# HGRN2 scan and gated MoE on one core: score matmuls cut to 64 by 64 tiles for all pairs, first pair as one MoE unit, one more pair turned by DMA, and a new order of steps

## The chip, the cores and the metric

The kernel runs on one core of one Trainium2 chip. The metric is the device time of one execution in microseconds (us), as the median of three runs. A profile of one execution gives the trace that is read here; its span runs from the program's first to its last instruction.

The engines are named as in the profile: PE is TensorE's matmuls, PEld its weight loads, DVE is VectorE, ACT is ScalarE, POOL is GpSimd and SP is SyncE, whose queue (SPq) issues nearly all transfers.

## The reference

Four batches, eight heads, 768 tokens, head width 48. A gated recurrence gives x, and a two-layer MoE-like block with h * cos(h) follows:

```python
def _attn_ref(q, k, v, f_logit):
    f = 1.0 / (1.0 + np.exp(-f_logit))
    state = np.zeros((B, H, D, D))
    for t in range(S):
        state = f[:, :, t, :, None] * state + einsum('bhd,bhe->bhde', k[:, :, t], v[:, :, t])
        y[:, :, t] = einsum('bhd,bhde->bhe', q[:, :, t], state)

def _moe_ref(x, w_in, w_out):      # x: 3072 x 384, w_in: 384 x 2048, w_out: 2048 x 384
    h = x @ w_in
    g = h * np.cos(h)
    return g @ w_out
```

Inputs and output are 32-bit floats.

## The kernel before

**Tiling.** The recurrence is done in chunks. 256 tokens of one batch are a *pair* (two chunks of 128 tokens): 12 pairs, three for each batch, n = 0 to 11. A token pair (even, odd) shares a partition, so that a chunk has 64 partitions. The MoE block works on *units* m of 256 tokens; `UNITS = [128, 128] + [256] * 11` lets pair 0 be units 0 and 1, so that pair n is unit n + 1 from n = 1 on.

**Steps.** `describe` makes a graph of named steps, each with a function that emits its instructions. For a pair n:

- `f`, `k`, `q`, `v` load the inputs on SP (halves `.0` and `.1`, four heads each, for pairs 0 and 1; f0.0 goes on ACT's queue).
- `ex`, `ln`, `fx`, `fy` (ACT), `ad` (POOL) make the log decays; `cum` (PE, L374 and L380) sums them along the tokens; `eb` and `ei` (ACT, L391 and L395) are the exponentials of the sums.
- `qa` (L341), `ka` (L351), `qm`, `km` (L404) scale q and k into the tile `qk`: on DVE or POOL for pairs 0 and 1, on POOL for the others. `vb` and `vt` (L197) cast and place v.
- `tq`, `tk` turn q and k for one half u of the heads. For pairs outside `TURN_QK = range(5, 12)` they are four PE transposes each (L435), and `qkt` (DVE or ACT) copies the result out of PSUM. For pairs in `TURN_QK` there is one step `tq{n}.{u}` on SP, a DMA transpose from `qk` to `qkt` (L424), and no copy.
- `sc` (PE, L456) are the scores; `am` (DVE, L461) masks them; `ps` (PE, L479) are the products k times v of the state, on 64 by 64 tiles; `st` and `sz` (DVE, L497 and L503) carry and decay the state.
- `y` and `yi` (PE, L531) give the pair's x, transposed; `xe` (ACT or DVE, L197) copies it out.

For a unit m: `h{m}.{j}{s}` (PE, L579) is a slice of the first product, six matmuls with 256 columns, or twelve with 128 columns for a unit of 128 tokens; `co` (ACT, L584) is the cosine and `g` (DVE, L561) the gate; `o{r}.{s}` (PE, L595) is a quarter of the second product for 128 tokens, four matmuls of 384 columns; `ot` copies it out and `out` stores it. The last store is split in two halves, `.0` and `.1`.

The weights come in four quarters each: `w0.i` (w_in) and `w1.i` (w_out) are loads of 768 KB on SP into a slot of the `g` pool, and `wc0.i`, `wc1.i` cast them on POOL or ACT.

`zf0` to `zf53` (PE, L264) are matmuls on zeros that fill TensorE's time at the start; their result is not used.

**Order.** Nothing is scheduled at run time. The string `ORDER` lists all steps with an engine letter (T PE, S ACT, V DVE, G POOL, Y SP) and the slots that their results take, e.g. `tk4.0:T` or `tq5.1:Y2`. `emit` goes through it and issues each step on its engine, so that every engine runs its own steps in that order, and waits by semaphores for what a step reads and for the last reader of the slot it writes. PSUM has four tiles of two banks, numbered 0 to 7 as slots; a step for scores or for h takes a whole tile. SBUF pools have the slot counts in `SLOTS` (three for `qk`, five for `qkt` and `g`). SP's queue is in order too: a load that waits for its slot holds all behind it.

**Scores before.** The step `sc` takes each of eight blocks (two head pairs a, two chunks g, two heads r). For a turned pair the 128 key tokens are cut in two: 16 matmuls with 64 stationary columns. For the others one matmul has all 128 stationary columns: 8 matmuls.

Of the kernel before, what the change touches and what calls it, by code (L numbers as in the profile page):

```python
# [41 lines left out]
zf18:T3 cum1.1:T3 zf19:T4 zf20:T4 zf21:T4 tq0.1:T0 cum1.0:T1 qm0.0:G zsz.2:G eb1.0:S1 vt0.3:S2
k1.0:Y ei1.0:S0 ex3:S zf22:T4 zf23:T4 zf24:T4 zf25:T4 zf26:T4 ps0.1:T4,5 ps0.0:T tk0.1:T v1:Y1 f2:Y0
qkt0.1:V0 eb1.1:S ln3:S0 ei1.1:S ka1.0:G q1.0:Y0 tq0.0:T ka1.1:G km1.1:G0 zvt.1:G vt0.0:S ad3:G1
vt0.1:G q1.1:Y vb1:S1 qkt0.0:V1 vt0.2:G zsz.1:G ex2:S w0.1:Y0 w0.0:Y1 k3:Y0 q3:Y1 w0.3:Y2 ln2:S1
vt1.2:S1 fy3:S zf27:T6 zf28:T6 zf29:T6 zf30:T6 zf31:T6 zf32:T6 sc0.0:T0 sz0.01:V2 sz0.00:V w0.2:Y3
ad2:G0 vt1.0:G km1.0:V vt1.3:G wc0.1:G am0.0:V0 zf33:T6 zf34:T6 yi0:T4 sc0.1:T2 am0.1:V1 st0.11:V
sz0.11:V3 wc0.0:G k2:Y1 zf35:T6 zf36:T6 zf37:T6 zf38:T6 ps1.1:T6,7 tk1.0:T0 ps1.0:T zf39:T1 zf40:T1
zf41:T1 cum3:T1 fy2:S ei3:S0 fx3:S ka3:G eb3:S2 vt1.1:S fx2:S km3.0:G1 qa3:G qm3.0:G km3.1:G qm3.1:G
w1.0:Y0 qa1.0:V st0.10:V qa1.1:V qm1.0:V wc0.2:G ka2:G q2:Y2 tk1.1:T2 zf42:T3 zf43:T3 y0:T3 tq1.0:T  # L50
xe0.1:S0 sz0.10:V st1.00:V st1.01:V qm1.1:V v2:Y1 zf44:T5 zf45:T5 zf46:T5 zf47:T5 zf48:T5 tq1.1:T
cum2:T1 sz1.00:V1 qkt1.0:V0 eb2:S0 xe0.0:S ei2:S1 qkt1.1:V1 km2.0:G0 km2.1:G zf49:T5 sc1.0:T4
sz1.01:V zf50:T0 zf51:T0 sc1.1:T2 h0.01:T0 st1.11:V sz1.11:V2 am1.1:V0 wc1.0:G qa2:G zf52:T6 zf53:T6
h0.00:T co0.0:S0 qm2.1:G am1.0:V1 h1.01:T2 h1.00:T co1.0:S1 y1:T6,4 yi1:T g0.0:V1 xe1.1:V1 st1.10:V
qm2.0:G vb2:G1 sz1.10:V g1.0:V4 w1.2:Y3 xe1.0:S tk3.0:T5 h2.01:T0 tq3.0:T w1.3:Y0 qkt3.0:V0 v3:Y0
f4:Y0 h2.10:T6 h2.00:T sc3.0:T4 tq3.1:T2 tk3.1:T h2.11:T wc1.2:G wc1.3:G vt2.1:G1 wc0.3:S vb3:G0
co2.0:S1 am3.0:V0 g2.0:V2 h2.20:T4 h2.21:T h0.11:T0 co2.1:S0 qkt3.1:S1 co2.2:S1 sc3.1:T2 w1.1:Y3
g2.1:V am3.1:V1 g2.2:V h0.10:T h1.11:T6 h1.10:T h2.30:T2 tk2.1:T4 tk2.0:T5 co0.1:S0 co1.1:S2 g0.1:V
g1.1:V h2.31:T o2.0:T0 co2.3:S0 tq2.1:T vt3.2:G2 vt3.1:G tq2.0:T o0.0:T1 o3.0:T6 o1.0:T7 qkt2.0:S2
vt2.0:S g2.3:V qkt2.1:V3 sc2.0:T2 ex4:S o3.2:T o0.2:T am2.0:V2 ln4:S1 ps2.0:T4 sc2.1:T2 vt2.3:G  # L60
ps2.1:T am2.1:V3 st2.01:V st2.00:V sz2.01:V1 sz2.00:V wc1.1:S f5:Y2 ex5:S ln5:S0 o1.2:T o2.3:T
o3.3:T o0.3:T o2.2:T q4:Y2 ps3.0:T4,5 ps3.1:T zsz.0:G vt2.2:G ad4:G0 yi2:T2,3 y2:T vt3.3:G sz3.01:V0
sz3.00:V o1.3:T cum4:T4 v4:Y0 vt3.0:G ad5:G0 fy4:S eb4:S0 st3.11:V fx4:S k4:Y1 fy5:S qa4:G qm4.0:G1
fx5:S ei4:S1 o0.1:T o2.1:T o3.1:T xe2.0:V1 st3.10:V sz3.10:V1 qm4.1:G sz3.11:V xe2.1:V ot2:V0
h3.00:T2 o1.1:T cum5:T0 ei5:S0 eb5:S2 k5:Y0 h3.01:T ot0:V1 vb4:G0 ka4:G y3:T4,5 yi3:T q5:Y1 h3.10:T0
h3.11:T co3.0:S0 xe3.0:V0 xe3.1:V ot1:V2 ot3:V3 co3.1:S2 g3.0:V4 h3.21:T4 h3.20:T co3.2:S1 h4.21:T6
h4.20:T g3.1:V ka5:G km4.0:G co4.2:S0 km4.1:G vt4.1:G2 qa5:G h4.11:T2 h4.10:T g3.2:V co4.1:S2
h4.31:T0 k6:Y2 qm5.1:G0 h4.30:T vt4.0:G vt4.2:G km5.1:G f6:Y1 v5:Y0 v6:Y1 f7:Y0 tq4.0:T4 tq4.1:T5
out3:Y tk4.0:T tk4.1:T co4.3:S1 g4.2:V2 h3.31:T6 h3.30:T qkt4.1:S0 qkt4.0:V1 g4.1:V o5.1:T4 co3.3:S0
o5.2:T o5.0:T o4.1:T5 g4.3:V g3.3:V ps4.1:T0,1 ps4.0:T st4.01:V st4.00:V sc4.1:T2 sc4.0:T6 am4.1:V0  # L70
am4.0:V1 sz4.00:V0 sz4.01:V qm5.0:G vt4.3:G st4.10:V tq5.1:Y2 sz4.10:V2 o5.3:T o4.2:T km5.0:G o4.0:T
o4.3:T ex6:S ln6:S0 vb6:G0 ad6:G0 ex7:S cum6:T2 y4:T3,6 tq5.0:Y3 yi4:T ot5:S3 st4.11:V sz4.11:V
vb5:G1 fx6:S ln7:S1 ei6:S0 eb6:S1 xe4.1:S1 o6.2:T4 out5:Y ad7:G0 ka6:G km6.0:G1 km6.1:G vt5.0:G2
vt5.1:G ps5.0:T2 ps5.1:T xe4.0:S st5.01:V sc5.0:T6 am5.0:V0 out0:Y k7:Y0 q6:Y1 q7:Y2 fy6:S fx7:S
f9:Y2 sc5.1:T0 cum7:T3 o6.3:T o6.1:T vt5.3:G h4.01:T6 h4.00:T st5.00:V am5.1:V1 sz5.01:V0 vt6.3:G1
qa6:G eb7:S0 ot4:S1 ka7:G ei7:S1 ps6.1:T3,5 ps6.0:T sz6.01:V1 sz5.00:V sz6.00:V v7:Y0 co4.0:S0
qm6.0:G h5.00:T0 h5.01:T co5.0:S1 vt5.2:S g4.0:V st6.11:V fy7:S h5.31:T2 h5.30:T o6.0:T y5:T6,7
yi5:T g5.0:V4 co5.3:S0 ot6:S3 tq6.0:Y0 xe5.1:S0 xe5.0:S f8:Y1 km7.0:G0 qa7:G km7.1:G qm7.1:G qm7.0:G
qm6.1:G h5.20:T0 h5.21:T st6.10:V sz6.10:V3 sz6.11:V g5.3:V tq7.1:Y2 tq6.1:Y3 vt6.2:S co5.2:S1
h5.10:T4 h6.20:T6 h6.21:T g5.2:V h5.11:T h6.10:T2 h6.11:T o7.2:T0 o8.2:T1 o7.0:T o8.3:T co6.2:S0  # L80
co5.1:S2 co6.1:S1 g6.2:V1 ex9:S g5.1:V out4:Y ln9:S1 sc6.0:T4 sc7.1:T6 g6.1:V am6.0:V0 ex8:S ln8:S0
fx8:S am7.1:V1 vt6.1:G vb7:G1 vt7.1:G2 vt6.0:S tq7.0:Y1 o7.3:T o7.1:T ps7.1:T4,5 ad9:G0 sc6.1:T2
ps7.0:T fx9:S ot7:V1 am6.1:V2 o8.1:T st7.00:V cum9:T6 o9.1:T0 o8.0:T sc7.0:T2 ad8:G1 cum8:T7
sz7.00:V0 am7.0:V3 q8:Y1 out6:Y o9.3:T o9.2:T ei9:S1 vt7.3:S fy9:S vt7.0:G eb8:S1 ei8:S0 fy8:S
eb9:S2 k8:Y0 out1:Y st7.01:V sz7.01:V v8:Y0 vt7.2:G qa8:G h6.01:T2 h6.00:T st7.10:V ot8:V3 sz7.10:V2
st7.11:V y6:T4,6 sz7.11:V xe6.0:S1 yi7:T1,7 yi6:T xe6.1:V y7:T o9.0:T xe7.1:V2 co6.0:S1 xe7.0:V
h7.31:T4 h6.31:T6 h6.30:T qm8.0:G0 ka8:G km8.0:G ot9:S2 v9:Y1 g6.0:V h8.21:T0 h7.30:T k9:Y2 vb8:G1
qm8.1:G co6.3:S2 vb9:G0 ka9:G tq8.0:Y0 q9:Y2 g6.3:V co7.3:S1 h8.20:T co8.2:S0 h7.20:T2 h7.21:T
h7.11:T6 co7.2:S2 h7.10:T g7.3:V4 h8.10:T4 out2:Y h8.11:T co7.1:S1 g8.2:V2 km8.1:G qa9:G f10:Y1
km9.0:G1 km9.1:G qm9.0:G co8.1:S0 g7.2:V h7.01:T0 h7.00:T o11.3:T2 o10.1:T3 g8.1:V k10:Y1 out8:Y  # L90
vt8.1:G2 f11:Y0 o11.1:T o10.3:T o12.3:T4 o10.2:T co7.0:S2 g7.0:V tq8.1:Y3 tq9.0:Y1 o12.0:T g7.1:V
ps8.1:T5 ex10:S ln10:S0 vt9.0:G1 ad10:G1 qm9.1:G ps9.1:T6,7 sc8.0:T0 ps9.0:T ps8.0:T am8.0:V1
o12.1:T o11.0:T cum10:T0 ex11:S fx10:S ln11:S1 ei10:S1 vt8.0:S eb10:S0 st8.00:V sz9.00:V1 st8.01:V
sz9.01:V st9.10:V sz8.01:V0 sz8.00:V o12.2:T o10.0:T st9.11:V o13.0:T6 ot10:S3 ot12:S0 o13.2:T
v10:Y1 ad11:G0 sz9.11:V3 sc9.0:T4 sc8.1:T0 cum11:T3 out12:Y o13.3:T o13.1:T o11.2:T am8.1:V3
am9.0:V0 sz9.10:V tq9.1:Y2 ka10:G vt8.3:G out10:Y km10.0:G0 vt8.2:G vt9.1:G km10.1:G ot11:V0 ei11:S0
eb11:S1 vt9.2:S vb10:S1 fx11:S yi8:T0,1 y8:T vt9.3:G xe8.0:S1 fy10:S q10:Y2 v11:Y0 out9:Y
ps10.0:T7,4 ps10.1:T sc9.1:T2 qa10:G k11:Y1 xe8.1:V qm10.0:G q11:Y1 am9.1:V1 st10.00:V st10.01:V
o14.1:T5 h8.01:T0 h8.00:T ot13:S3 co8.0:S1 sz10.01:V0 sz10.00:V st10.10:V o14.2:T h8.30:T2 h8.31:T
g8.0:V ka11:G h9.31:T6 h9.30:T co8.3:S2 tq10.0:Y0 o14.0:T y9:T0,1 yi9:T g8.3:V co9.3:S1 fy11:S  # L100
xe9.0:S2 o14.3:T qm10.1:G km11.1:G1 km11.0:G vb11:G0 zqk.2:G zsp.2:G h9.01:T2 h9.00:T co9.0:S2
ot14:S2 st10.11:V sz10.10:V1 g9.3:V1 out14:Y out11:Y sz10.11:V xe9.1:V h9.11:T6 h9.10:T co9.1:S1
h9.20:T0 h9.21:T g9.0:V g9.1:V h10.10:T4 tq10.1:Y1 co9.2:S2 out7:Y g9.2:V h10.00:T2 h10.11:T
h10.20:T6 vt11.3:S1 co10.1:S1 g10.1:V4 h10.01:T co10.0:S2 o16.1:T0 h10.21:T o16.0:T g10.0:V o16.2:T
o16.3:T sc10.0:T2 co10.2:S1 out13:Y ot16:S3 g10.2:V sc10.1:T4 ps11.1:T1 vt11.0:G vt10.3:G2 ps11.0:T
qa11:G vt11.1:S qm11.1:G st11.01:V tq11.1:Y2 sz11.01:V2 am10.0:V0 am10.1:V1 h10.31:T6 o17.3:T0
# [611 lines left out]
```

## Time and profile before

| | us |
|---|---|
| median of 3 runs | 182.84 (182.62 to 184.4) |
| the profiled execution: span | 180.9 |
| PE busy, of the span | 172.6 (95%) |
| DVE, ACT, POOL busy | 134.6, 130.7, 109.2 |

The page gives one execution. It cuts the span into 40 slices and shows for each engine how busy it was, in tenths; PEclk is the TensorE clock that was granted:

```
PE   7899789999999999999999999999999999999992
DVE  5259988897595988897999697689888894356260
ACT  3985987777878899989997899769768452473221
POOL 4229899999969986989665977890798000000000
DMA  5999999999999944986899999559927500110313
```

DMA is the mean busy share of the core's 16 DMA engines. The start of the work (some 25 us) is spent on loads and on pairs 0 and 1; the MoE matmuls (L579 and L595) fill most of the rest. All matmuls of the first product (L579) are busy for 68.1 us and those of the second (L595) for 68.9 us in the trace.

### The profile page before, as it was taken

What the parts mean: (1) busy time and instruction counts of PE and PEld (TensorE: products, weight loads), DVE (VectorE), ACT (ScalarE), POOL (GpSimd) and SP (SyncE); (2) the same over time, 40 slices, a digit from 0 to 9 for tenths busy, and PEclk for the clock granted to TensorE, in tenths of its full rate; (3) what the DMA queues carried; (4) which work ended last, traced back from release to release, by engine and by line L of the source; (5) the groups of instructions that cost most, each with busy time, mean ns of one, the idle gap of its engine ahead of it and who ended that gap; (6) DMA issues with size and microseconds to landing.
All of it is one profiled execution on the core that took longest, in us unless ns stands there. A gap on an engine that the chain in (4) does not pass through costs nothing.

```text
span 180.9 us, 5814 instructions
## 1 busy us (share of the span) xinstructions
PE 172.6 (95%) x2460; PEld 123.9 (69%) x2464; DVE 134.6 (74%) x206; ACT 130.7 (72%) x187; POOL 109.2 (60%) x139
## 2 busy tenths in 40 slices
PE   7899789999999999999999999999999999999992
...
DVE  5259988897595988897999697689888894356260
ACT  3985987777878899989997899769768452473221
POOL 4229899999969986989665977890798000000000
...
DMA  5999999999999944986899999559927500110313
GB/s 149 261 261 276 343 320 341 250 318 284 301 265 233 274 83 123 252 210 145 122 180 308 173 267 278 124 131 251 203 92 182 100 4 0 43 47 4 130 43 131
...
## 3 DMA queue, kind: packets, MB, share of 16 engines
...
q8 instruction: 19, 0.31, 0.7%
q10 hardware_dynamic: 672, 0.30, 0.6%
q14 instruction: 7, 0.06, 0.1%
...
## 4 chain that ended last, share of the span: by engine, by line
PE 81%; DMA 7%; ACT 3%; DVE 3%; SPq 2%; issue 1%; ACTq 0%
PE ps L595 35%; PE ps L579 33%; PE ps L531 5%; DMA f<-in_f_logit_dram 4%; PE ps L456 4%; DMA v<-in_v_dram 3%; SPq L296 2%; PE ps L479 2%; DVE g L561 1%; PE ps L435 1%; PE ps L374 1%; DVE am L461 1%; PE ps L264 1%; ACT f L344 0%; ACT f L329 0%
## 5 line engine op out<-in xcount | busy, mean ns | idle before, releaser
L561 DVE TENSOR_TENSOR g<-ps,co 128x1024 bf16<-128x1024 f32 x48 | 57.4, 1220 | 18.0 <-ACT co L584 16.7
L595 PE MATMUL ps<-w_out_bf,g 128*128 128x384 bf16 x384 | 68.9, 326 | 0.0
L579 PE MATMUL ps<-x,w_in_bf 128*128 128x256 bf16 (+1 forms) x624 | 68.1, 264 | 0.5 <-DVE x L197 0.4
L584 ACT ACTIVATE co<-ps,halfpi 128x1024 bf16<-128x1024 f32 x48 | 52.7, 1113 | 19.8 <-PE ps L579 19.5
L579 PEld LDWEIGHTS <-w_in_bf 128*128 128x128 bf16 x624 | 56.3, 98 | 9.2 <-DVE x L197 0.6
L595 PEld LDWEIGHTS <-g 128*128 128x128 bf16 x384 | 36.1, 98 | 21.4
L461 DVE TENSOR_TENSOR am<-ps,pmask 128x1024 bf16<-128x1024 f32 x24 | 28.7, 1218 | 5.2 <-PE ps L456 4.9
L404 POOL TENSOR_TENSOR qk<-k,bi 128x384 bf16<-128x384 f32 x22 | 22.0, 1008 | 5.4 <-ACT bi L391 4.7
L404 POOL TENSOR_TENSOR qk<-q,b 128x384 bf16<-128x384 f32 x21 | 20.8, 1000 | 2.7 <-DVE q L338 2.1
L197 POOL COPY vt<-vb 64x384 bf16<-64x384 bf16 x33 | 16.7, 507 | 1.6
L264 PE MATMUL ps<-zero 128*128 128x512 bf16 x50 | 14.6, 412 | 1.5 <-DVE zero L203 1.2
L503 DVE TENSOR_TENSOR sz<-ps,b 64x192 bf16<-64x192 f32 x40 | 14.1, 354 | 2.5 <-PE ps L479 1.6
L363 POOL TENSOR_TENSOR sp<-ls 128x384 bf16<-128x384 f32 x10 | 10.3, 1028 | 7.8 <-ACT ls L333 6.1
L341 POOL TENSOR_TENSOR q<-f,q 128x384 f32<-128x384 f32 x10 | 10.0, 998 | 8.0 <-DMA q<-in_q_dram 5.8
L329 ACT ACTIVATE f<-f 128x768 f32<-128x768 f32 (+1 forms) x14 | 10.4, 746 | 4.4 <-DMA f<-in_f_logit_dram 4.4
L497 DVE TENSOR_TENSOR ps<-ps,sz 64x192 f32<-64x192 f32 x32 | 11.7, 367 | 2.2 <-PE ps L479 1.1
L351 POOL TENSOR_TENSOR k<-k,f 128x384 f32<-128x384 f32 (+1 forms) x12 | 11.1, 931 | 3.4 <-DMA k<-in_k_dram 3.4
L197 ACT COPY ot<-ps 128x384 f32<-128x384 f32 (+1 forms) x14 | 6.1, 453 | 8.7 <-PE ps L595 8.7
L197 ACT CAST x<-ps 128x384 bf16<-128x384 f32 x12 | 5.5, 479 | 6.0 <-PE ps L531 6.0
L456 PE MATMUL ps<-qkt 48*64 48x128 bf16 (+1 forms) x304 | 8.7, 218 | 1.1 <-ACT x L197 0.8
L197 DVE CAST x<-ps 128x384 bf16<-128x384 f32 x12 | 6.4, 553 | 4.1 <-PE ps L531 3.9
L264 PEld LDWEIGHTS <-zero 128*128 128x128 bf16 x54 | 4.8, 103 | 5.9 <-issue 1.9
...
## 6 DMA issues: line engine op xcount, KB each, us to landing
...
```

The lines of the kernel that those rows point to most:

```text
L197: (nc.scalar.copy if e == "ACT" else eng(e).tensor_copy)(out=o, in_=i)
L264: G.step(f"zf{i}", ("PE",), lambda e, dump=dump: nc.tensor.matmul(dump.ap, lhsT=zero[:, 0:128], rhs=zero, start=True, stop=True), writes=[ ...
L351: eng(e).tensor_mul(out=w.ap[:, :, 0, :], in0=w.ap[:, :, 0, :], in1=t.ap[:, :, 0, :])
L404: G.step(f"{nm}{n}.{u}", ("POOL", "DVE") if cut else ("POOL",), lambda e, u=u, j=j, src=src, dec=dec: eng(e).tensor_mul(out=qkp[u][j].ap[: ...
L456: nc.tensor.matmul(o[t0:t1, r, 2 * a + g, :].rearrange("p (e n) -> p e n", e=2), lhsT=wide[s, t0 // 64, :] if turned else wide[s].rearrang ...
L461: G.step(f"am{n}.{u}", ("DVE",), lambda e, u=u, sc=sc: nc.vector.tensor_mul(out=am[u].ap.rearrange("p r b n -> p (r b) n"), in0=sc.ap.rear ...
L497: nc.vector.tensor_add(out=view()[s], in0=view()[s], in1=S0.ap[s, :, r, :])
L503: eng(e).tensor_mul(out=new.ap[s, :, r, :].rearrange("p (u a) n -> p u a n", u=2), in0=view()[s].rearrange("p (u a) n -> p u a n", u=2), i ...
L561: nc.vector.tensor_mul(out=o.rearrange("p b (n e) -> p b n e", e=2), in0=ph.ap.rearrange("p (b e n) -> p b n e", e=2, n=64), in1=co.ap.rea ...
L579: nc.tensor.matmul(ph.ap[:, i * T:(i + 1) * T].rearrange("p (g t) -> p g t", t=C), lhsT=w_in_bf[:, kk, f0:f0 + 128], rhs=xa[:, :, kk, :], ...
L584: G.step(f"co{m}.{j}", ("ACT",), lambda e, ph=ph, co=co: nc.scalar.activation(out=co.ap, in_=ph.ap, func=AF.Sin, bias=halfpi), reads=[ph], ...
L595: nc.tensor.matmul(po.ap[:, 0:DM], lhsT=gT.ap[:, j, i * C:(i + 1) * C], rhs=w_out_bf[:, j, :], start=(po.first and j == 4 * s), stop=(po.f ...
```

## The change

Four things are changed.

1. `sc` always cuts the key tokens in two: 16 matmuls with 64 stationary columns for every pair. Before this held for pairs 5 to 11; pairs 0 to 4 change.
2. `UNITS = [256] * 12`: pair 0 is one unit of 256 tokens, and pair n is unit n. The first product of pair 0 is 8 steps of 6 matmuls with 256 columns and no longer 8 steps of 12 with 128.
3. `TURN_QK = range(4, 12)`: pair 4 is turned by two DMA transposes from SP. Its four PE steps `tq4`, `tk4` and two copies `qkt4` go.
4. `ORDER` is new from end to end, and `ZEROS` goes from 54 to 52. Among the rest, the order of loads on SP, the place of each DMA transpose, and the engines of some copies are other ones.

```diff
-TURN_QK = range(5, 12)
-UNITS = [128, 128] + [256] * 11
+TURN_QK = range(4, 12)
+UNITS = [256] * 12
...
-ZEROS = 54
+ZEROS = 52
...
             def scores(e, u=u, sc=sc):
                 o = sc.ap.rearrange("p (r b n) -> p r b n", r=2, n=C)
-                cuts = ((0, 64), (64, 128)) if turned else ((0, 128),)
                 for a in range(2):
                     for g in range(2):
                         for r in range(2):
-                            for t0, t1 in cuts:
-                                s, wide = slice(64 * r, 64 * r + D), qkv(u)[:, 1, a, g]
-                                nc.tensor.matmul(o[t0:t1, r, 2 * a + g, :].rearrange("p (e n) -> p e n", e=2),
-                                                 lhsT=wide[s, t0 // 64, :] if turned else wide[s].rearrange("p e n -> p (e n)"),
-                                                 rhs=qkv(u)[s, 0, a, g, :, :],
+                            for h in range(2):
+                                s = slice(64 * r, 64 * r + D)
+                                nc.tensor.matmul(o[64 * h:64 * h + 64, r, 2 * a + g, :].rearrange("p (e n) -> p e n", e=2),
+                                                 lhsT=qkv(u)[s, 1, a, g, h, :], rhs=qkv(u)[s, 0, a, g, :, :],
                                                  start=(a == 0 and g == 0), stop=(a == 1 and g == 1))
```

The loads on SP up to pair 4, before and after (ORDER's words for that engine, without their slots):

```diff
-f0.1 k0.0 k0.1 f1.1 f1.0 q0.1 q0.0 v0 f3 k1.1 k1.0 v1 f2 q1.0 q1.1 w0.1 w0.0 k3 q3 w0.3 w0.2 k2 w1.0 q2 v2 w1.2 w1.3 v3 f4 w1.1 f5 q4
+f0.1 f1.1 k0.1 v0 q0.1 k0.0 f1.0 f3 q0.0 k1.0 v1 q1.1 f2 q1.0 k1.1 w0.0 w0.1 k3 q3 w0.2 w0.3 q2 w1.2 k2 w1.3 w1.0 v3 v2 w1.1 f4 f5 q4
```

The new order around the first MoE step, where pair 10 is prepared, and at the end:

```diff
...
+zf45:T1 zf46:T1 tk1.1:T qkt1.1:S0 sz0.10:V qkt1.0:V2 ps1.1:T zf47:T1 sc1.0:T4 st1.00:V st1.01:V
+xe0.1:S0 am1.0:V2 fx3:S cum2:T1 eb2:S2 xe0.0:V fx2:S ei2:S2 w0.0:Y1 wc0.0:G zf48:T6 zf49:T6 zf50:T6
+zf51:T6 sc1.1:T4 am1.1:V0 h0.01:T2 h0.00:T sz1.00:V0 y1:T6,1 co0.0:S2 sz1.01:V st1.11:V yi1:T
+xe1.0:S1 st1.10:V w0.1:Y0 wc0.1:G xe1.1:V sz1.10:V0 h0.11:T4 k3:Y2 ka3:G h0.10:T h1.01:T6 sz1.11:V
+co0.1:S0 g0.0:V0 h1.00:T km3.1:G0 tk3.1:T0 co1.0:S3 g0.1:V q3:Y0 qa3:G qm3.1:G tq3.1:T qm3.0:G
+h1.10:T2 km3.0:G w0.2:Y1 wc0.2:S w0.3:Y2 wc0.3:G h1.11:T co1.1:S1 qkt3.1:V3 sc3.1:T4 g1.0:V3
+h1.20:T0 h1.21:T co1.2:S0 h0.31:T6 h0.30:T co0.3:S2 am3.1:V3 q2:Y1 qa2:G qm2.0:G2 w1.2:Y4 wc1.2:G
+k2:Y2 h0.21:T4 g1.1:V h0.20:T co0.2:S3 tq3.0:T2 tk3.0:T g1.2:V g0.3:V h1.31:T0 h1.30:T co1.3:S1
...
+ei11:S0 eb11:S1 o13.1:T ad10:G0 cum10:T3 vt9.0:S ot13:S2 ei10:S2 o11.1:T4 o11.0:T ot12:V1 am8.0:V3
+sc9.0:T0 am9.0:V2 sc8.1:T6 am8.1:V0 k10:Y1 out12:Y k11:Y2 eb10:S0 sc9.1:T2 o10.3:T o11.2:T o11.3:T
+vt8.0:G o10.0:T v11:Y0 fx11:S fy10:S fy11:S qa10:G vb10:G1 vt8.3:G yi9:T7 yi8:T1,0 ka10:G km10.0:G0
...
+g7.0:V h8.30:T0 h8.31:T vb11:G2 qm10.0:G vt10.2:G1 ka11:G q11:Y1 km11.0:G1 h7.31:T2 qa11:G qm11.1:G
+vt11.3:G2 vt11.2:G km11.1:G tq11.1:Y1 tq10.0:Y2 qm10.1:G qm11.0:G km10.1:G h7.30:T tq10.1:Y3
+tq11.0:Y4 out11:Y xe9.1:S h9.01:T6 co8.3:S0 g8.3:V2 h9.00:T h8.11:T4 out13:Y h8.00:T0 h8.01:T
...
+o15.2:T ot15:S1 out15:Y o14.0:T o17.1:T6 sc10.0:T4 ps10.0:T7,2 am10.0:V0 sc10.1:T0 ps10.1:T o17.0:T
...
+o21.3:T ot21:S2 o22.1:T4 o22.3:T ot20:S1 out20:Y out16:Y g11.2:V o22.2:T g11.0:V o22.0:T ot22.1:S1
+out22.1:S o23.0:T7 o23.1:T ot22.0:V o23.3:T o23.2:T ot23.0:V3 out22.0:S ot23.1:S out14:Y out21:Y
+out23.1:Y out23.0:S
...
```

142 lines of the change are left out of this document (62 added, 80 removed).

## The prediction

> **What bounds the kernel now.** I read the page's first part, then the busy time by stage, then the chain of waits.
>
> ```profile
> PE 172.6 (95%) x2460; PEld 123.9 (69%) x2464; DVE 134.6 (74%) x206; ACT 130.7 (72%) x187; POOL 109.2 (60%) x139
> ```
>
> ```profile
> 0.00:24.84 24.84, 20.52 (x256) 1.00 1.09 261
> 24.84:33.92 9.08, 8.41 (x154) 1.00 1.08 335
> 33.92:177.61 143.69, 143.67 (x2052) 1.00 0.71 167
> 177.61:180.87 3.26, 0.00 (x0) 1.00 0.38 128
> ```
>
> The columns of the stages are the stretch, its length, TensorE's busy time, granted clock, DMA share and GB/s. From 33.92 us to its last matmul at 177.61 TensorE is idle for 0.02 us, at full clock. So whatever is taken from TensorE's list after its first MoE matmul shortens the span one for one, unless a wait appears in its place. Ahead lies the start, until the first MoE matmul (24.84); behind lies a tail of 3.26. The span is 180.87; the three runs have a median of 182.84, so 1.97 lies outside the span. I keep that and sum against the span.
>
> **The prices on TensorE.** Each piece of the chain is start, length, line, matmuls.
>
> ```profile
> 36.06 0.33 PE ps L456 x8
> 36.39 2.77 PE ps L579 x42
> ...
> 49.60 0.90 PE ps L531 x56
> ...
> 56.42 6.66 PE ps L579 x60
> 63.08 0.89 PE ps L435 x16
> ```
>
> ```profile
> 89.78 0.57 PE ps L456 x32
> 90.35 1.41 PE ps L595 x8
> 91.76 0.24 PE ps L479 x16
> 92.00 0.23 PE ps L456 x16
> 92.23 0.12 PE ps L479 x16
> 92.35 0.76 PE ps L595 x4
> ```
>
> ```profile
> 171.74 5.86 PE ps L595 x36
> 177.61 0.02 issue
> 177.63 0.03 ACT ot L197
> 177.65 0.19 issue
> 177.84 0.33 ACT ot L197
> ```
>
> - A second-MoE step (four matmuls, L595) costs 5.86 / 9 = 0.65. Behind smaller work it costs 0.76 (at 92.35): a change of the array's shape costs 0.11.
> - A first-MoE step on 256 columns (six, L579): (6.66 - 0.11) / 10 = 0.655. On 128 columns (twelve): the piece of 42 is three such and one of six, (2.77 - 0.11 - 0.655) / 3 = 0.67.
> - A score step of 16 matmuls, 64 by 64, costs 0.23 between state products (92.00: same shape, no change to pay), and two cost 0.57 behind L595, which is 2 x 0.23 and the change. The form with 8 matmuls costs 0.33 with one change, 0.22 without.
> - The sixteen transposes of a pair (four steps, L435) cost 0.89.
>
> **What the change does to TensorE's list.** Counted over the new order behind its first MoE step h0.01:
> - Pair 4's four transpose steps go: -0.89.
> - Eight steps of 128 columns become eight of 256: 8 x (0.67 - 0.655) = -0.12.
> - Scores of pairs 2 to 4 (six steps; pairs 0 and 1 lie in the start): 16 small matmuls for 8 larger ones, 6 x 0.01 = +0.06. Halving the tile doubles the matmuls and each takes half as long, so it gains nothing by itself.
> - Changes of shape: state products and scores now have one shape and often stand side by side. Counting neighbours of unlike shape behind h0.01 gives 52 before and 41 after: 11 x 0.1 = -1.1.
>
> Together -2.0. By these prices the old list behind h0.01 makes 150.9, against 152.8 from 24.8 to 177.6: 1.9 of waits and filler, all before 34 us. The new list makes 148.9.
>
> A rule of the Trainium skill speaks against the 64-column form: the page TensorEngine Tiling, section Restrictions and Gotchas, says that column tiling excludes the fast weight load.
>
> ```profile
> L456 PEld LDWEIGHTS <-qkt x304: 92/107/110, 13.8 to 147.5; 48*64 48x64 bf16 x112, 48*128 48x128 bf16 x40
> ```
>
> Lowest, median and highest ns: the 224 narrow loads have the 107, the 80 wide ones the 92. If loads stood in line, a narrow score step would need 16 x 0.107 = 1.7. It takes 0.23, so loads and matmuls of different quarters overlap. By that rule alone the ten steps would cost some 10 x (1.7 - 0.7) = 10 us more; the trace does not bear it out, and the sum takes nothing for it.
>
> **The start.** In both orders the same fifteen loads stand ahead of the first weights in SyncE's queue, only permuted: eleven halves of f, k and q of pairs 0 and 1, and v0, v1, f3, f2.
>
> ```profile
> 10.51 7.11 DMA f<-in_f_logit_dram
> ...
> 24.84 0.78 PE ps L579 x12
> ```
>
> f2 landed at 17.62 with two halves behind it. At 0.75 each (384 KB at the 261 GB/s of the first stage are 1.5) the last half lands near 19.1 in either order: q1.1 before, k1.1 after. From k1.1 the new order goes: decay product on GpSimd, km1.1, sz0.10, the copy qkt1.0, st1.00, st1.01 and am1.0 on VectorE, xe0.0, then h0.01.
>
> ```profile
> L497 DVE TENSOR_TENSOR ps<-ps,sz 64x192 f32<-64x192 f32 x4 | 1.5, 367 | 0.2
> L503 DVE TENSOR_TENSOR sz<-ps,b 64x192 bf16<-64x192 f32 x4 | 1.4, 354 | 0.1
> L197 DVE COPY qkt<-ps 128x1024 bf16<-128x1024 bf16 x2 | 1.3, 673 | 0.0
> L461 DVE TENSOR_TENSOR am<-ps,pmask 128x1024 bf16<-128x1024 f32 x1 | 1.2, 1225 | 0.4 <-PE ps L456 0.4
> L404 DVE TENSOR_TENSOR qk<-q,b 128x384 bf16<-128x384 f32 x2 | 1.1, 551 | 0.0
> ```
>
> VectorE's part is 0.55 + 0.35 + 0.67 + 2 x 0.37 + 1.23 = 3.5; the ends on either side are taken like the 0.55 row, and waits between engines at 0.4: 19.1 + 5.0 = 24.1. Before, the stretch from 19.1 to the first MoE matmul took 5.7, and a sum like this one does not see every wait. So I take 0 for the start, not -0.7, with bounds of -0.7 and +0.7. The weights are the cover that could go: w0.0 (786 KB at the second stage's 335 GB/s, 2.3) lands near 21.4 and its cast is GpSimd's next work, ready near 23, 1 us ahead of its use.
>
> **Waits behind the start.** The first MoE unit now needs all four quarters of w_in early. In the new order w0.2 waits in SyncE's queue until the cast wc0.0 frees its staging buffer, and w0.3, q2, w1.2, k2 stand behind it. It is fourth behind w0.0: w0.1 2.3, k3 and q3 1.2 to 1.5 each, itself 2.3, which is 21.4 + 7.3 = 28.7; ScalarE casts it behind a cosine, ready at 31 to 32. TensorE comes to its first use, h1.20, after eight steps of 0.655, one pair's sums (0.90), two transposes (0.45) and a score step: 24.8 + 7.0 = 31.8. So 0 to 0.5 is lost there. am1.0, sc3.1's copy and two late `cum` steps can cost 0.3 each: 1.5 in all, against the 1.9 of before.
>
> What is new are pair 4's two DMA transposes, and how near each transpose lies to its scores. First what the trace says of the fourteen DMA transposes of qk (from SyncE's issue), then GpSimd's and ScalarE's work between 112 and 138 us:
>
> ```profile
> DMA to landing us min/median/max: 3.0/3.2/5.1
> ```
>
> ```profile
> L197 POOL COPY vt<-vb 64x384 bf16<-64x384 bf16 x8 | 4.0, 500 | 0.4
> L404 POOL TENSOR_TENSOR qk<-q,b 128x384 bf16<-128x384 f32 x4 | 4.0, 997 | 0.2
> L404 POOL TENSOR_TENSOR qk<-k,bi 128x384 bf16<-128x384 f32 x4 | 4.0, 1002 | 0.2
> ...
> L197 POOL CAST vb<-v 128x768 bf16<-128x768 f32 x1 | 0.8, 832 | 0.0
> ```
>
> ```profile
> L395 ACT ACTIVATE bi<-ps 128x384 f32<-128x384 f32 x2 | 1.0, 490 | 2.4 <-PE ps L380 2.4
> L395 ACT ACTIVATE b<-ps 128x392 f32<-128x392 f32 x2 | 1.0, 490 | 0.0
> ```
>
> The tightest I could find late in the order is tq10.1. Its clock starts at cum10: four activations of 0.49 and the hand-overs make 2.4 to qa10; from there to km10.1 GpSimd has 12 products of 1.00, 4 copies of 0.50 and 2 casts of 0.83 in one row, 15.7, and 0.05 idle at each of 18: 16.5; then 3.2 to land: 22.1. TensorE from cum10 to sc10.1 has 14 steps of 0.65, 16 of 0.655, 4 score steps of 0.23, and the sums of two pairs (0.90 each with L531's row) with cum10, state products and changes: 22.9. Cover 0.8; at the longest landing seen it is -1.1. Walked so, tq5.1 and tq8.1 have 0.7, tq7.1 1.0, the other twelve 1.5 or more. What queues behind a late one is TensorE itself, and the next loads on SyncE. I expect one or two to be late, 0.7 together, since 3.2 is a median. Waits then come to 2.2, +0.3 on before; bounds -0.4 (none late) to +4 (below).
>
> **The tail.** The last output copy is split over VectorE (.0) and ScalarE (.1), but both write one tile and the second waits for the first: 0.02 + 0.35 + 0.33 = 0.70 and a hand-over, against 0.57 before (177.61 to 178.17). +0.2. Its halves go out on two queues as before.
>
> Sum: -2.0 + 0 + 0.3 + 0.2 = -1.5: a span of 179.4, and 182.84 - 1.5 = 181.3. Pair 4's two copies out of PSUM go too (0.67 on VectorE, no more than twice that on ScalarE); nothing of TensorE waited there, so they count nothing.
>
> **Rivals.**
> 1. *All of it arrives.* The start ends at its walked 24.1, no transpose is late: -2.0 - 0.7 - 0.1 + 0.2 = -2.6, or -2.1 with the start unchanged: 180.2 to 180.8, say 180.5. For it: 12 of 16 covers are long, and the trace before had 14 transposes without one wait of TensorE on them. Against: four covers under 1.1.
> 2. *The transposes take TensorE's place* (slower). Late landings at tq5.1, tq7.1, tq8.1 and tq10.1 each stop TensorE, and with it the state products whose end GpSimd waits for, so that the next cover shrinks as well. If each lands 1.5 over the median, 4 x 1.5 less the covers (3.2) is 2.8; if every stop comes back once through GpSimd it is 5.6; I take 4 in place of the 0.7, some +3.5: 184.8, and SyncE's loads behind them may add. It decides once those four land on average 1.5 over the median; the 5.1 in the row shows that 1.9 over happens.
> 3. *The tile doesn't do what its name says*: by the weight-load rule above, some +10, 191. The rows of the pairs that have it already speak against it.
>
> **How the numbers follow.** About 1% (1.8 us) is what a measurement of this kernel can tell from no change. My forecast of 181.3 is within 1%: 0.42. Rival 1, faster by over 1%: 0.36. Rival 2 or any other slip of its size, slower by over 1%: 0.21; rival 3: 0.01. The range takes in rival 1 down to 180.1 (start -0.7 and one late transpose fewer) and rival 2 up to 185.7; beyond lie a tenth on each side. The likeliest case's own range is 181.0 to 182.5.
>
> **What would show it.** Right: L435 with 64 matmuls; first L579 between 24.1 and 25.5; 16-matmul score pieces of 0.23 beside L479; about 2 us of TensorE idle behind h0.01; a tail of about 3.4. Wrong: TensorE waiting on DMA qkt for over 1.5 in all (rival 2); first L579 past 25.6; or score pieces over 0.4 (rival 3).

## The result, and the profile after

The changed kernel takes 0.9867 of the time of the kernel before (95% interval 0.9828 to 0.9907): some 180.4 us against 182.81. The median of its four executions, 182.12, contains two in which TensorE was granted a clock of 0.988 to 0.989, and the ratio, here and below, leaves out executions over 1.5% longer than the kernel's fastest. The profiled execution has a span of 178.20, 2.67 less than 180.87, with 1.78 around it.

The first line of the page of the changed kernel, and its stages (stretch, length, TensorE's busy time, then weight loads, VectorE, ScalarE and GpSimd, clock, DMA share, GB/s), cut at the first MoE matmul and at the last matmul's start, as before:

```profile
PE 170.5 (96%) x2475; PEld 122.8 (69%) x2478; DVE 136.6 (77%) x206; ACT 127.2 (71%) x179; POOL 112.9 (63%) x145
```

```profile
0.00:25.19 25.19, 21.20 (x287) 11.06 (x291) 19.27 (x48) 17.91 (x38) 17.51 (x31) 1.00 1.00 241
25.19:33.90 8.71, 8.31 (x138) 6.95 (x139) 8.43 (x13) 7.48 (x8) 7.33 (x7) 1.00 1.06 344
33.90:174.97 141.07, 140.97 (x2052) 104.75 (x2050) 108.57 (x146) 101.53 (x133) 88.10 (x107) 1.00 0.77 179
174.97:178.20 3.23, 0.00 (x0) 0.00 (x0) 0.36 (x1) 0.32 (x1) 0.00 (x0) 1.00 0.18 61
```

The start is 0.35 longer (25.19 against 24.84), the tail 0.03 shorter, and from the first MoE matmul to the last matmul's start it is 149.78 in place of 152.77: all of the gain, 2.99, lies there. This stretch in one row, before and after, and the filler (matmuls on zeros) that the kernel before had in it:

```profile
24.84:177.61 152.77, 152.08 (x2206) 113.27 (x2206) 117.78 (x158) 111.30 (x144) 94.73 (x114) 1.00 0.73 177
```

```profile
25.61 0.43 PE ps L264 x2
```

```profile
25.19:174.97 149.78, 149.29 (x2188) 111.70 (x2188) 117.00 (x158) 109.01 (x141) 95.43 (x114) 1.00 0.79 188
```

TensorE's idle time goes from 0.69 to 0.49, the 0.43 of filler are gone, and the rest of its busy time goes from 151.65 to 149.29: 2.4 less work.

The chain of waits shows the prices unchanged (start, length, line, matmuls; L455 are scores, L477 state products, L593 the second MoE product), and the tail's two copies:

```profile
48.81 0.35 PE ps L455 x16
...
65.77 0.37 PE ps L477 x32
66.14 0.46 PE ps L455 x32
66.59 2.71 PE ps L593 x16
...
137.66 0.12 PE ps L477 x16
137.77 0.23 PE ps L455 x16
138.01 0.12 PE ps L477 x16
...
174.99 0.37 DVE ot L197
175.36 0.02 issue
175.38 0.32 ACT ot L197
```

A score step of the pairs whose tile is new costs what one of pair 10 costs: 0.23 beside state products (two of pair 4 at 66.14, one of pair 10 at 137.77), 0.35 with one change of shape (pair 2 at 48.81). The two copies at the end do follow one another, 0.73 in all against 0.56.

Of the transposes on TensorE 64 matmuls are left, and among its waits behind the start one has a size, the cast of w_in's third quarter; no row names a DMA transpose:

```profile
L435 PE MATMUL ps<-ident,qk 128*128 128x128 bf16 x64 | 5.7, 220 | 1.4 <-DVE qk L404 1.3
```

```profile
PE ps L577 <- ACT w_in_bf L197: 0.3, 1, 0.3
```

### The profile page after: what moved, and what is told of

Read it like the earlier page. It is cut to its first block, busy times and chain, and to the rows that moved or that the text cites. A ratio compares the mean times of both kernels' runs of the same rounds, so it can differ in the third digit from the quotient of the medians.

```text
span 178.2 us, 5848 instructions
## 1 busy us (share of the span) xinstructions
PE 170.5 (96%) x2475; PEld 122.8 (69%) x2478; DVE 136.6 (77%) x206; ACT 127.2 (71%) x179; POOL 112.9 (63%) x145
## 4 chain that ended last, share of the span: by engine, by line
PE 84%; DVE 6%; SPq 4%; DMA 3%; issue 1%; ACT 1%; DVEq 0%
PE ps L593 36%; PE ps L577 35%; PE ps L529 5%; SPq L296 4%; PE ps L455 3%; DMA k<-in_k_dram 3%; DVE am L459 2%; PE ps L477 2%; DVE qk L404 1%; PE ps L435 1%; PE ps L374 1%; DVE ps L495 1%; ACT w_in_bf L197 1%; DVE x L197 1%; PE ps L264 0%
## 5 line engine op out<-in xcount | busy, mean ns | idle before, releaser
L559 DVE TENSOR_TENSOR g<-ps,co 128x1024 bf16<-128x1024 f32 x48 | 58.0, 1222 | 20.0 <-ACT co L582 17.1
L593 PE MATMUL ps<-w_out_bf,g 128*128 128x384 bf16 x384 | 68.0, 326 | 0.0
L577 PE MATMUL ps<-x,w_in_bf 128*128 128x256 bf16 x576 | 66.9, 273 | 0.4 <-ACT w_in_bf L197 0.3
L577 PEld LDWEIGHTS <-w_in_bf 128*128 128x128 bf16 x576 | 55.5, 98 | 9.0 <-ACT w_in_bf L197 0.5
L593 PEld LDWEIGHTS <-g 128*128 128x128 bf16 x384 | 36.2, 98 | 21.5
L197 POOL COPY vt<-vb 64x384 bf16<-64x384 bf16 x40 | 20.6, 516 | 3.1 <-ACT vb L197 1.3
L404 POOL TENSOR_TENSOR qk<-k,bi 128x384 bf16<-128x384 f32 x20 | 19.9, 1001 | 0.7
L351 POOL TENSOR_TENSOR k<-k,f 128x384 f32<-128x384 f32 (+1 forms) x13 | 11.8, 909 | 6.0 <-DMA k<-in_k_dram 3.5
L197 POOL CAST vb<-v 128x768 bf16<-128x768 f32 x10 | 8.6, 856 | 1.5 <-DMA v<-in_v_dram 1.5
L455 PEld LDWEIGHTS <-qkt 48*64 48x64 bf16 x384 | 6.2, 106 | 4.5 <-issue 2.4
L455 PE MATMUL ps<-qkt 48*64 48x128 bf16 x384 | 8.8, 220 | 0.5 <-DVE am L459 0.2
```

Of the source, the lines that this page charges most:

```text
L197: (nc.scalar.copy if e == "ACT" else eng(e).tensor_copy)(out=o, in_=i)
L351: eng(e).tensor_mul(out=w.ap[:, :, 0, :], in0=w.ap[:, :, 0, :], in1=t.ap[:, :, 0, :])
L404: G.step(f"{nm}{n}.{u}", ("POOL", "DVE") if cut else ("POOL",), lambda e, u=u, j=j, src=src, dec=dec: eng(e).tensor_mul(out=qkp[u][j].ap[: ...
L455: nc.tensor.matmul(o[64 * h:64 * h + 64, r, 2 * a + g, :].rearrange("p (e n) -> p e n", e=2), lhsT=qkv(u)[s, 1, a, g, h, :], rhs=qkv(u)[s, ...
L559: nc.vector.tensor_mul(out=o.rearrange("p b (n e) -> p b n e", e=2), in0=ph.ap.rearrange("p (b e n) -> p b n e", e=2, n=64), in1=co.ap.rea ...
L577: nc.tensor.matmul(ph.ap[:, i * T:(i + 1) * T].rearrange("p (g t) -> p g t", t=C), lhsT=w_in_bf[:, kk, f0:f0 + 128], rhs=xa[:, :, kk, :], ...
```

## The experiments

Ratios are to the kernel before, run beside each kernel on the same chip, with 95% intervals. Its spans in these 78 executions lay between 180.5 and 182.2.

### The changed kernel again

> The changed kernel once more, as the standard for the other runs. Expected 0.983 to 0.991 of the kernel before. In its trace TensorE's list behind the first MoE matmul should take 148.9 by the prices of the prediction, and the waits behind it 0.7 again (0.69 in the first trace: 0.39 ahead of h1.20, 0.16 ahead of sc3.1). Theory 1, no transpose is ever late: the span stays at 178.2, or moves with the start alone. Theory 2, the small covers (0.21 us at tq10.1, 0.54 at tq8.1 in the first trace) are used up in some executions: a span near 179.2 with TensorE waiting on qkt in front of sc10.1 or sc8.1.

Measured: 0.9899 (0.9875 to 0.9923), profiled span 178.8, spans of its executions 178.8 to 180.1, and one of 183.0 at a clock of 0.990. List and tail are as in the first trace. Over the 148.9 it has 175.57 - 25.38 - 148.9 = 1.3, where the first trace had 0.9 and 0.7 was expected; the 0.4 between the traces are a hole at 122 us (last section). No transpose was late in this trace either, so it decides nothing between the two theories.

> The changed kernel again, as the standard on the same chip as the next two: 0.986 to 0.992 of the kernel before, span 178.2 to 180.1. My theory of its spread: where loads or transposes land later than in the first trace, GpSimd's chain shifts and TensorE waits in the middle (pairs 5 to 10); a span above 179 should show such waits between 60 and 140 us, none of them before 25.

Measured: 0.9943 (0.9918 to 0.9969), over the range expected. Its twelve spans lie between 178.8 and 182.2, and the profiled one is among the longest, 181.5. TensorE's waits in it that the first trace did not have:

```profile
PE ps L529 <- ACT ot L197: 1.5, 1, 1.5
...
PE ps L455 <- DMA qkt<-qk: 1.1, 1, 1.1
```

The second is tq10.1, in front of sc10.1: GpSimd had come 2.1 later to km10.1 than in the first trace, and the transpose took 4.7 to land and not 3.4. The first leads to ScalarE (start, length, line, and in brackets the idle time before it and its releaser):

```profile
69.79 0.84 ACT L329 ACTIVATE f<-f 128x768 f32<-128x768 f32 x1 [2.28 <-DMA f<-in_f_logit_dram]
70.54 0.46 ACT L197 COPY ot<-ps 128x384 f32<-128x384 f32 x1
70.89 0.84 ACT L333 ACTIVATE ls<-f 128x768 f32<-128x768 f32 x1
71.64 0.47 ACT L197 COPY ot<-ps 128x384 f32<-128x384 f32 x1
```

Load f7 landed at 69.7. The exponential ex7 stood waiting for it at the head of ScalarE's queue, and ot5 and ot4, whose data were long there, stood behind; yi4 on TensorE needed ot4's bank. Over the 148.9 this trace has 178.22 - 25.23 - 148.9 = 4.1. So one and the same kernel has 0.9, 1.3 and 4.1 over its list in three traces (idle time of TensorE: 0.5, 0.7 and 3.1), all of the difference between 60 and 141 us: late landings in this trace, the hole in a0_again, and none of it in the start.

### One part of the change alone

**b_tile.** The kernel before with its scores all in 64 by 64 tiles:

```diff
-                cuts = ((0, 64), (64, 128)) if turned else ((0, 128),)
+                cuts = ((0, 64), (64, 128))
...
-   lhsT=wide[s, t0 // 64, :] if turned else wide[s].rearrange("p e n -> p (e n)"),
+   lhsT=wide[s, t0 // 64, :],
```

> The kernel before with one thing changed: scores of pairs 0 to 4 in 64 by 64 tiles, the order of steps as it was. My theory: the tile itself gains nothing (16 matmuls of half the size), only places where scores stand beside state products lose a change of the array's shape (3 behind the first MoE step): 0.2 us less, ratio 0.997 to 1.001, and the sixteen-matmul pieces of pairs 2 to 4 take 0.23 to 0.25. Rival, the tile is what makes the change faster: at least 0.1 per step, 1 us or more, ratio 0.994 or less. Rival, weight loads stand in line: 10 us more.

Measured: 0.9973 (0.9962 to 0.9984), profiled span 180.5. Its chain has pair 2's first step, with one change of shape, and pair 9's between state products:

```profile
43.40 0.35 PE ps L456 x16
...
91.77 0.23 PE ps L456 x16
```

A narrow step of pair 2 costs what one of pair 9 does and the change. The gain is 0.5 us (0.3 to 0.7), somewhat more than the 0.2 forecast and the 0.3 that three changes of shape make at 0.11; neither rival is borne out.

**b_turn and b_turn2.** b_tile with pair 4 turned by DMA, the two transposes at one or the other of two places of SyncE's queue (the first line with a plus below is b_turn, the second b_turn2):

```diff
-TURN_QK = range(5, 12)
+TURN_QK = range(4, 12)
-... km4.1:G ... k6:Y2 ... f7:Y0 tq4.0:T4 tq4.1:T5 tk4.0:T tk4.1:T ... qkt4.1:S0 qkt4.0:V1
+... km4.1:G tq4.0:Y1 tq4.1:Y0 ... k6:Y2 ... f7:Y0
+... km4.1:G ... k6:Y2 ... f7:Y0 tq4.0:Y1 tq4.1:Y0
```

> b_tile and pair 4 turned by two DMA transposes behind km4.1, the rest of the order as before. My theory: 0.89 us of transposes leave TensorE's list and nothing else is late, since the transposes land near 64 and the scores start near 67: 0.9 less than b_tile, 1.1 less than before, ratio 0.993 to 0.996. Rival, the two transposes hold SyncE's queue by 1.25 each and the loads of pairs 6 and 7 or a later transpose become late: no gain over b_tile, or slower, with waits of TensorE on qkt between 70 and 100 us.

Measured: 1.0229 (1.0193 to 1.0266). The profiled execution, 183.7, is the only one of six at full clock, the others were granted 0.982 to 0.991; so its 3.2 us over b_tile's profiled span are the better measure. It is the rival's mechanism, loads held back, though TensorE does not wait where it said, on qkt. SyncE's queue (start, length of the issue, line, transfer):

```profile
51.07 1.40 SPq L296 DMA_DIRECT2D q<-in_q_dram  x1
59.37 2.71 SPq L424 DMA_TRANSPOSE qkt<-qk  x2
62.13 0.61 SPq L296 DMA_DIRECT2D k<-in_k_dram  x1
```

Between 52.5 and 59.4 nothing is issued: tq4.0 waits for GpSimd's product, and k6, f6, v5, v6 and f7 stand behind it. In b_tile k6 was issued at 52.55. Some ten microseconds behind the hold TensorE pays, at cum6 and at ps5.0:

```profile
PE ps L374 <- POOL sp L363: 1.8, 1, 1.8
...
PE ps L479 <- ACT b L395: 1.1, 1, 1.1
```

> As b_turn, but the two transposes stand in SyncE's queue where pair 4's first PE transposes stood in the order: behind the loads k6, f6, v5, v6 and f7 and ahead of out3. In b_turn they stood ahead of k6 and held it from 52.5 to 62.1 us. My theory: it was the place in the queue that cost the 4.2 us over the kernel before, not the transposes: now 0.9 less than b_tile, ratio 0.991 to 0.994. Rival, the two transposes cost DMA time that the loads of pairs 6 and 7 need wherever they stand: ratio over 1.000, with TensorE waiting at cum6 or ps5.0 again.

Measured: 0.9984 (0.9962 to 1.0007), profiled span 180.1. TensorE waits neither at cum6 nor at ps5.0, so the place was what cost in b_turn. But the forecast gain shows only in part of the executions: seven have spans of 179.9 to 180.6 (b_tile's ten: 180.5 to 181.0), five lie between 181.0 and 181.6. On the mean turning pair 4 gave the old order nothing. What the five waited for, no trace shows.

### One part undone

**a_noturn.** The changed kernel with pair 4 turned on TensorE:

```diff
-TURN_QK = range(4, 12)
+TURN_QK = range(5, 12)
-tq4.0:Y3 ... tq4.1:Y2 ... o4.1:T0 o5.2:T1 ... co3.3:S3
+o4.1:T0 tq4.0:T2 tk4.0:T tq4.1:T3 tk4.1:T o5.2:T1 ... co3.3:S3 qkt4.0:S3 qkt4.1:S2
```

> The changed kernel with pair 4 turned on TensorE again: four transpose steps behind o4.1 and two copies on ScalarE, and two transposes fewer on SyncE. Theory of the prediction: 0.89 us come back to TensorE's list and nothing else changes: 0.9 more than the changed kernel, ratio 0.991 to 0.997. Rival, from b_turn2, where turning pair 4 by DMA gave nothing on the mean: the two transposes take back in later landings what they save, so the time is the changed kernel's (within 0.3 us) and its executions spread less.

Measured: 0.9994 (0.9967 to 1.002) beside 0.9943 for the changed kernel on the same chip: 0.9 us (some 0.3 to 1.6), the price. Its smallest span, 179.9, stands 1.1 over the changed kernel's 178.8. At full clock its spans reach from there to 182.9, as widely as the changed kernel's (178.8 to 182.2), so the spread is not pair 4's. Part of the 0.9 is another cost of mine: the two copies on ScalarE hold ex6 back, and cum6 came 0.4 late.

**a_split.** The changed kernel with eleven steps of the second product put between scores and state products, for example

```diff
-ps4.1:T ... sc4.0:T6 am4.0:V1 sc4.1:T4 ... o5.3:T o5.1:T
+ps4.1:T o5.3:T ... sc4.0:T6 am4.0:V1 sc4.1:T4 ... o5.1:T
```

> The changed kernel with eleven second-MoE steps moved between scores and state products that stood side by side: the same instructions, 63 changes of the array's shape behind the first MoE step in place of 41. My theory: each change costs TensorE 0.08 to 0.1 us, 1.9 in all: ratio 0.999 to 1.002, and TensorE's span from the first L577 to the last matmul 1.9 longer. Rival, the changes of shape cost nothing by themselves and the gain of 1.1 that I gave them came from elsewhere: same time as the changed kernel (0.987 to 0.992).

Measured: 1.0086 (1.0069 to 1.0103), profiled span 182.6. From the first MoE matmul (25.21) to the last matmul (179.34) it is 154.1, 4.3 over the first trace of the changed kernel. The price of the changes is seen in its chain at each cut: a step of the second product alone between others costs 0.76 where 0.65 would be no change.

```profile
66.62 0.37 PE ps L477 x32
66.99 0.76 PE ps L593 x4
67.75 0.57 PE ps L455 x32
```

That is 0.11 for each change, more than I had expected, and 22 of them are 2.4. TensorE's idle time is 1.7 where the first trace had 0.5, which I had not expected either: the state products and scores reach VectorE later, and TensorE waits for VectorE's part of the chain, most of it at cum10:

```profile
PE ps L374 <- DVE sz L501: 0.7, 1, 0.7
```

The remaining 0.7 stand in TensorE's busy time, and I have not traced them to a step. So the rival falls, and placing scores beside state products is worth its changes of shape and some of VectorE's slack besides.

### The cover of the transposes

**a_late.** `tq10.1` behind `out11`:

```diff
-tq10.1:Y3 tq11.0:Y4 out11:Y
+tq11.0:Y4 out11:Y tq10.1:Y3
```

> The changed kernel with tq10.1 two places later on SyncE, behind tq11.0 and out11. In the changed kernel it landed 0.21 us before sc10.1; here it should land near 139, 1.4 late. Theory (rival 2 of the prediction): TensorE stops for all of it, 1.4 us in one place and none comes back later, since GpSimd has nothing left to do for it: 1.0 to 2.0 us more than the changed kernel. Rival: part of it is hidden, for TensorE's list behind has slack elsewhere: under 0.5.

Measured: 1.0027 (0.9993 to 1.0062), over the 0.990 that the changed kernel has on the mean of its three some 1.2%, 2.3 us. Part of that is clock: six of its ten executions were granted 0.982 to 0.991, two of them among the five in the ratio. The four at full clock have spans of 180.5 to 183.5, the changed kernel's nineteen such 178.2 to 182.2. Nor does the trace show a loss of this size at the place: there TensorE lost 0.23, since in that execution it came to sc10.1 only at 139.6. It had waited 1.0 at ps8.1 for a GpSimd that was late from ka9 on, by a late load of k9, ahead of anything the edit touches. So this order is slower, but that the late transpose costs it what the theory says is not shown.

**a_early.** Three transposes with more cover, both halves of the last copy on ScalarE:

```diff
-out7:Y ... tq9.0:Y3 tq9.1:Y4 tq8.1:Y0
+out7:Y tq9.1:Y4 ... tq9.0:Y3 tq8.1:Y0
-q11:Y1 ... tq11.1:Y1 tq10.0:Y2 qm10.1:G qm11.0:G km10.1:G ... tq10.1:Y3
+q11:Y1 tq10.0:Y2 ... tq11.1:Y1 qm10.1:G km10.1:G tq10.1:Y3 qm11.0:G
-ot23.0:V3 ... ot23.1:S
+ot23.0:S3 ot23.1:S
```

> The changed kernel with more cover for three of its transposes (tq9.1 two transfers earlier, tq10.0 ahead of tq11.1, and GpSimd's km10.1 ahead of qm11.0 so that tq10.1 follows at once) and with both halves of the last copy on ScalarE. Theory 1, the transposes never stop TensorE in the changed kernel: same time as it, 0.99 of the kernel before, and executions spread as widely as its own (178.2 to 180.1 us of span so far). Theory 2, the small covers are used up in some executions: the spread shrinks to 1 us or less and the ratio falls to 0.983 to 0.987. The tail (last matmul's start to the end) should be 3.0 to 3.1 in place of 3.23, since two copies on one engine overlap.

Measured: 0.9879 (0.9858 to 0.9901), spans 178.1 to 179.4: between the two theories, and the intervals don't separate it from the changed kernel. The tail is 3.13 and its copies take 0.54:

```profile
175.77:178.90 3.13, 0.00 (x0) 0.00 (x0) 0.00 (x0) 0.54 (x2) 0.00 (x0) 1.00 0.19 63
```

With tq9.1 moved ahead, v10 and out9 slid back and sc8.1 had to wait for its transpose (0.36 in all): cover was moved rather than won.

### Towards a better order

**a_cast.** `co1.0:S3 ... wc0.2:S` becomes `wc0.2:S co1.0:S3`.

> The changed kernel with the cast of w_in's third quarter (wc0.2, ScalarE) ahead of the cosine co1.0 and not behind it. My theory: the 0.39 us that TensorE waits ahead of h1.20 go, since the quarter landed at 29.3 and ScalarE stood idle until co1.0's start at 30.3; co1.0 ends 0.5 later, and its gate has 1.2 us until h0.31 needs the bank: 0.3 to 0.4 us less than the changed kernel. Rival, TensorE takes the wait back at the next bank (h0.31 waits for g1.0): no difference.

Measured: 0.9871 (0.985 to 0.9893) beside 0.9899 (0.9875 to 0.9923): not separated. In the trace the 0.39 ahead of h1.20 is gone and 0.33 stands ahead of h1.31, which waits for the gate g1.2 on VectorE. The rival named the right thing, one bank later.

**a_best.** The cast, two copies from VectorE to ScalarE, and the tail:

```diff
-xe0.1:S0 ... xe0.0:V ... xe1.1:V ... co1.0:S3 ... wc0.2:S
+xe0.1:S0 xe0.0:S ... xe1.1:S ... wc0.2:S co1.0:S3
-ot23.0:V3 ... ot23.1:S ... out23.1:Y out23.0:S
+ot23.0:S3 ot23.1:S out23.1:S ... out23.0:Y
```

> The changed kernel with wc0.2 ahead of co1.0 (as in a_cast), the copies xe0.0 and xe1.1 on ScalarE in place of VectorE, and both halves of the last copy on ScalarE. My theory: from 12.7 to 35 us VectorE's chain sets the pace (19.27 of 25.19 and 8.43 of 8.71 us busy), and the wait that a_cast removed came back at h1.31 because VectorE's gates were late. With two copies of 0.55 off it: the first L577 0.2 earlier, no wait at h1.20 nor at h1.31, the tail 0.1 shorter: 0.6 to 0.8 us less than the changed kernel, ratio 0.983 to 0.987. Rival, ScalarE takes the place of VectorE (its cosines start later by the two copies): same time as the changed kernel.

Measured: 0.99 (0.9874 to 0.9926) beside 0.9943 (0.9918 to 0.9969), 0.8 us less than the changed kernel (some 0.1 to 1.5), as forecast in sum; the ratio itself lies above the range forecast, as the changed kernel's does on this chip. By its parts it is not: the first L577 came at 25.15, no 0.2 earlier. The profiled execution was again a long one, 181.7, with the same two waits as the changed kernel's long one (1.31 at yi4 behind f7, 1.82 at sc10.1). The wait at h1.31 is still there (0.33), so ScalarE's later cosines took back that part.

**a_best2.** Four moves at those two waits:

```diff
-v6:Y0 tq4.0:Y3 ... tq4.1:Y2 ... f7:Y0
+v6:Y0 f7:Y0 tq4.0:Y3 ... tq4.1:Y2
-k10:Y1 out12:Y k11:Y2 ... v11:Y0
+k10:Y1 v11:Y0 out12:Y k11:Y2
-q11:Y1 ... tq11.1:Y1 tq10.0:Y2 qm10.1:G qm11.0:G km10.1:G ... tq10.1:Y3
+q11:Y1 tq10.0:Y2 ... tq11.1:Y1 qm10.1:G km10.1:G tq10.1:Y3 qm11.0:G
```

> a_best with four moves at the places where its long execution waited: load f7 ahead of tq4.0 (its landing near 69.5 had held ex7, ot5 and ot4 on ScalarE, and yi4 1.3 us on TensorE), load v11 ahead of out12 and k11, tq10.0 ahead of tq11.1, and GpSimd's km10.1 ahead of qm11.0 (tq10.1 had held sc10.1 for 1.8). My theory: late landings are what makes executions of the changed kernel differ, so these two waits go, spans lie between 178 and 179.7 and the ratio falls by 0.3 to 0.6% against a_best's 0.990: 0.983 to 0.987. Rival: the transfers moved ahead delay others (tq4, k11, out1), and the waits turn up at the next small cover (sc8.1, cum6 or ps8.1): 0.988 to 0.992.

Measured: 0.9865 (0.984 to 0.989), spans 178.0 to 179.4, where a_best had 178.1 to 181.7 at full clock. Both waits are gone: f7 lands at 63.2, and tq10.1 2.3 us ahead of its scores. One is left, 0.85 at ps8.1, where GpSimd had waited 2.15 for load k8:

```profile
110.75 0.69 PE L477 MATMUL ps<-vb,qk 64*64 64x48 bf16 x48 [0.68 <-POOL qk L404]
```

Theory and rival are both right in part: the spread falls, and the next late load shows. It is below the kernel before by 1.1 to 1.6%; against the changed kernel (0.9867 to 0.9943) it was not run on one chip.

## Why the prediction was right, and where it was not

The forecast of 181.3 is 0.9916 of 182.84. The three measurements gave 0.9867, 0.9899 and 0.9943: on both sides of it. Over all 22 executions of the changed kernel the mean span is 180.3, over the 78 of the kernel before 181.2. The first measurement, 180.4, lies below the likeliest case's own range and with rival 1 (180.5), whose sum of -2.6 the first trace met with -2.67, though by other terms, which is luck:

| term | forecast | first trace |
|---|---|---|
| TensorE's list behind h0.01 | -2.0 | -2.4 |
| start | 0 (walked: -0.7) | +0.35 |
| waits and filler behind it | +0.3 | -0.6 |
| tail | +0.2 | 0.0 |

**The list** holds in its parts, by four runs: the unchanged prices in the trace, 0.9 for pair 4's transposes (a_noturn, with the reservation made there), 0.4 at most for the tile itself (b_tile), 0.11 for a change of shape (a_split). Its totals were short: 150.9 where the trace before has 151.65 of work, and 148.9 for 149.29. So the 1.9 that I had read as waits and filler before were 0.69 and 0.43. The list gained 0.4 more than forecast; 0.1 of it is the price of a change of shape, taken as 0.1, and the rest I have not traced to a step. The weight-load rule (the Trainium skill, TensorEngine Tiling, section Restrictions and Gotchas) does not set the time here: b_tile has 160 more narrow loads in place of 80 wide ones, and a shorter span.

**The waits** were forecast at 2.2, and the three traces have 0.9, 1.3 and 4.1 over the list's 148.9: a spread with the forecast inside it and near its mean, though no trace has it. The step that failed is that I took one landing time, 3.2, for all executions and a fixed 0.7 for what it leaves. The median landing of the transposes is 3.6, 3.9 and 4.5 in the three traces, the longest 5.2, 5.6 and 6.3. Landings of one and the same transpose differ by up to 2 us (tq5.1: 3.3 in the first trace, 5.2 in a0_third) and shift GpSimd's chain, so the waits are a distribution. tq10.1, named as the tightest, had 0.21 in the first trace (forecast 0.8) and was the late one in the two longest, a0_third's and a_best's. tq8.1 had 0.54 (0.7) and stopped TensorE in a_noturn (0.8), a_early and a_best (0.3 to 0.4). tq5.1 was late once, by 0.25 in a_late, and tq7.1 never; their covers in the first trace, 1.84 and 1.83, were more than the 0.7 and 1.0 that I had walked, but tq5.1's was 0.8 in a0_again and 0.7 in a0_third. tq6.0, which I had among those of 1.5 or more, had 0.98. The other large late thing was not a transpose and not on my list: load f7 ahead of ex7, with ot4 behind it. Rival 2 therefore had the right mechanism (TensorE stops, and GpSimd's shift carries it on), at a smaller price than its 3.5 in the executions seen. The wait for w0.2 came as walked: landed at 29.3 (28.7), cast ready at 32.8 (31 to 32), 0.39 lost.

**The start** was walked along the wrong path. k1.1 landed at 19.00 (19.1), but what followed from it did not end last. The chain of the first trace leaves VectorE with qm1.0 and runs over TensorE's own list: tq1.0, ps1.0, tq1.1, the four matmuls on zeros zf43 to zf46 (one record is missing), tk1.1 and ps1.1.

```profile
19.23 0.93 DVE qk L404
20.17 0.04 issue
20.21 0.40 PE ps L435 x4
20.61 0.24 PE ps L477 x16
20.85 0.33 PE ps L435 x4
21.18 0.05 issue
21.23 0.81 PE ps L264 x3
22.04 0.22 PE ps L435 x4
22.27 0.30 PE ps L477 x16
22.57 0.36 DVE ps L495
...
25.19 1.47 PE ps L577 x12
```

These 2.4 us from qm1.0 to st1.00 are the step that failed: I had walked VectorE's steps from km1.1 on, and TensorE's had only a share of the 0.4 for waits, so by my sum st1.00 begins at 21.6 at the latest and not at 22.57. From st1.00 on it is the sum as I made it. That km1.1 was not on the path shows beside a0_third. First VectorE's km1.1 and st1.00 in the first trace, and GpSimd's product at that time, then the same in a0_third:

```profile
20.08 1.35 DVE L404 TENSOR_TENSOR qk<-k,bi 128x384 bf16<-128x384 f32 x1
...
22.56 0.77 DVE L495 TENSOR_TENSOR ps<-ps,sz 64x192 f32<-64x192 f32 x2 [0.27 <-PE ps L477]
```

```profile
19.93 1.08 POOL L363 TENSOR_TENSOR sp<-ls 128x384 bf16<-128x384 f32 x1 [0.19 <-ACT ls L333]
```

```profile
20.11 0.55 DVE L404 TENSOR_TENSOR qk<-k,bi 128x384 bf16<-128x384 f32 x1
...
22.59 0.77 DVE L495 TENSOR_TENSOR ps<-ps,sz 64x192 f32<-64x192 f32 x2 [1.07 <-PE ps L477]
```

```profile
20.11 1.41 POOL L363 TENSOR_TENSOR sp<-ls 128x384 bf16<-128x384 f32 x1 [0.34 <-ACT ls L333]
```

In a0_third km1.1 took the 0.55 that I had given it. VectorE then waited 1.07 for ps1.1 in place of 0.27, and the first MoE matmul came at 25.23 and not at 25.19. The zeros held tk1.1 back: it started at 21.88, and km1.1 was done at 21.43 in the first trace and at 20.66 in a0_third. What the start gains without them, no run shows.

The two products lengthen each other: where GpSimd's begins 0.15 ahead, VectorE's takes 1.35 in place of 0.55, and where both begin together, GpSimd's takes 1.41 in place of 1.08. The Trainium skill (SBUF — State Buffer, section SBUF: two separate sides) says that VectorE's operations with two SBUF inputs and GpSimd's take turns on one pair of ports, whoever starts first holding it for the whole instruction. The two traces agree in the main: in the first km1.1 ends 0.4 after GpSimd's product, and in a0_third GpSimd's product ends 0.9 after km1.1, though which of them began first is not to be seen there.

**The tail.** The copies cost 0.17 more as forecast; the last stores landed 0.2 sooner, which I had taken as equal. a_early shows 0.1 to be had.
